# One partial product is copied into another's PSUM bank, where the second accumulates upon it; an addition on VectorE goes

## The chip, the cores and the metric

The kernel runs on one core of one Trainium2 chip. The metric is device time in microseconds (us): 2280.09 us is the median of three runs before the change (2279.85 to 2280.32). The core's engines are TensorE (PE in the rows; its loads of stationary operands are PEld), VectorE (DVE), ScalarE (ACT), GpSimd (POOL), and SyncE (SP), which issues the transfers. Each engine runs its own instructions in the order in which they were written and waits on semaphores for the others.

## The reference

The work is channel attention followed by a gated feed-forward layer, on 4 batches of 6080 tokens with 256 channels; the hidden width is 2048.

```python
qn = q / (norm(q, axis=1) + 1e-06);  kn = k / (norm(k, axis=1) + 1e-06)
s = kn.transpose(0, 2, 1) @ qn / tau          # 256 x 256 for each batch
a = softmax(s)                                # rows, in float32
x = (v @ a).reshape(B * S, 256)
h = x @ w_in                                  # 256 -> 2048
g = h * (1 / (1 + exp(-1.702 * h)))
out = g @ w_out                               # 2048 -> 256
```

The weights `w_in` and `w_out` arrive as float64 and are turned into float32 on the chip.

## The kernel before, in words

For each batch the kernel first forms the 256 x 256 attention matrix from q and k (class `Attention`; the next batch's is built while the present one is multiplied), multiplies it into `w_in` (`weights`, line 582), and then only has to form V x (a w_in) for the tokens. The tokens of a batch are cut into 12 chunks of 512 (the last has 448), the hidden width into 4 groups of 512. One chunk with one group is a **unit** (`unit`, line 684); there are 4 x 12 x 4 = 192.

All matrices are split into a high and a low part of a reduced float32 format (`F32R`), and each product is a sum of three matmuls: high x high, low x high, high x low. So a **product** is 2 x 3 = 6 matmuls with 256 columns, into the two halves of one PSUM bank (`product`, line 695).

V x W is done by a scheme with seven products in place of eight, M1 to M7. Their partial sums live in three kinds of banks: X (two of them in turn, `psX0` and `psX1`), Y and Z (one each). M1 opens X; M6, M5 and M3 are accumulated upon it in that order, and after M1, M6 and M5 ScalarE takes a copy of X to SBUF (`snap`: tiles `s1`, `u2`, `u4`). M2 opens Z. M7 opens Y and M4 accumulates upon it. Four quadrants of the hidden layer follow:

- first (c11): `s1` + Z, added by VectorE into `h1`, then the gate (Gelu) on ScalarE in SBUF (g11);
- second: X after M3, gated directly from PSUM (g12);
- third and fourth (c22, c21): Y + `u4` and Y + `u2` into `h2`, each then gated in SBUF.

Then `parts` (line 745) splits the gated `h1` and `h2` into `gh` (a cast, by ScalarE for `h1`, by VectorE for `h2`) and `gl` (a subtraction on VectorE), and eight groups of three 512-column matmuls into the output banks `ps_o` multiply them by `w_out` (line 776). Below, "output groups" are these.

The first batch differs: units run in pairs of chunks, and between them the weights of the next group are read, turned to float32 on VectorE (`to_float32`, line 285) and multiplied by the attention matrix. This is the start-up, to about 170 us into the span. `weights` there puts its two halves (`ps_w`) one after the other into the same bank, and the second waits until ScalarE has copied the first (`w1`).

The order on every engine is made by a planner (`Plan.order`, line 85): each operation is a node with an engine, an assumed cost, its predecessors and a due time, and each engine takes the ready node with the smallest due time. Slots (banks and tiles) are reused in the order in which the program asked for them. Whatever changes costs, predecessors or due times of a few nodes therefore moves instructions on all engines.

Of the kernel before, what the change touches and what calls it, by code (L numbers as in the profile page):

```python
# [15 lines left out]
ALU = mybir.AluOpType  # L16
# [4 lines left out]
P = 128  # L21
# [3 lines left out]
NCH = 512  # L25
# [138 lines left out]
def act(n, psum=False, pointers=0):  # L164
    return (165 if psum else 190) + 0.833 * n + 93 * pointers


def dve(n):
    return (151 + n) / 0.96
# [10 lines left out]
def channel_attention_then_glu(  # L180
# [10 lines left out]
    nc = tc.nc  # L191
# [21 lines left out]
    g = Plan()  # L213

    def sbuf(slot, shape, dtype=F32, name=None):
        return g.buf(slot, lambda: sb.tile(list(shape), dtype, tag=slot, name=name or slot))
# [4 lines left out]
    def bank(slot, name=None):  # L221
        return g.buf(slot, lambda: ps.tile([P, NCH], F32, tag=slot, name="ps_" + (name or slot)))
# [3 lines left out]
    ones = sb.tile([P, P], F32, name="ones")  # L226
# [7 lines left out]
    def two(ap, w):  # L234
        return ap.rearrange("p (a n) -> p a n", a=2)[:, :, :w]
# [6 lines left out]
    def cast(dst, src, n, deps, uses, due, psum=False):  # L242
        return g.add("ACT", act(n, psum), lambda: nc.scalar.copy(dst(), src()), deps, uses, due)  # L243
# [4 lines left out]
    def tt(dst, a, b, op, n, deps, uses, due):  # L248
        return g.add("DVE", dve(n), lambda: nc.vector.tensor_tensor(dst(), a(), b(), op=op), deps, uses, due)  # L249
# [329 lines left out]
    P1, P2, P3, P5, P7, P6, P4 = range(7)  # L579
# [98 lines left out]

    marks = []
    outs = {}

    def unit(W, V, b, c, grp, count, chunk_no):
        D = len(marks)
        due = 45.0 * D
        o, w = chunks[c]
        hw = w // 2
        wh, wl, w_ok = W
        vh, vl, v_ok = V  # L690
        X = bank(f"psX{D % 2}", "X")
        Y = bank("psY", "Y")
        Z = bank("psZ", "Z")

        def product(m, into, begin, due, deps):
            def fn():
                for a in range(2):
                    dst = into()[:, a * HALF : a * HALF + hw]
                    for n, (l, r) in enumerate(((wh, vh), (wh, vl), (wl, vh))):
                        nc.tensor.matmul(  # L700
                            dst, lhsT=l()[:, m, a, :], rhs=r()[:, m, :hw],
                            start=begin and a == 0 and n == 0, stop=True, skip_group_check=True,
                        )

            return g.add("PE", 6 * hw * 0.4427, fn, [*deps, *w_ok, v_ok[m]], [wh, wl, vh, vl, into], due)

        def snap(name, dep, due):
            s = sbuf(name, [P, 2, HALF], F32)
            n = cast(lambda: s()[:, :, :hw], lambda: two(X(), hw), w, [dep], [X, s], due, psum=True)
            return s, n  # L710

        h1 = sbuf(f"h1{D % 2}", [P, 2, NCH], F32, "h1")
        h2 = sbuf("h2", [P, 2, NCH], F32)
        left = lambda h: h()[:, :, :hw]
        right = lambda h: h()[:, :, hw:w]

        def gate(dst, src, deps, uses, due, psum):
            return g.add(
                "ACT", act(w, psum), lambda: nc.scalar.activation(dst(), src(), AF.Gelu_apprx_sigmoid),  # L719
                deps, uses, due,  # L720
            )

        m1 = product(P1, X, True, due, [])
        marks.append(m1)
        s1, s1n = snap("s1", m1, due + 4)
        m2 = product(P2, Z, True, due + 6, [])
        m6 = product(P6, X, False, due + 15, [s1n])
        u2, u2n = snap("u2", m6, due + 19)
        c11 = tt(lambda: left(h1), lambda: two(Z(), hw), lambda: s1()[:, :, :hw], ALU.add, w,
                 [s1n, m2], [Z, s1, h1], due + 11)  # L730
        g11 = gate(lambda: left(h1), lambda: left(h1), [c11], [h1], due + 24, False)
        m5 = product(P5, X, False, due + 27, [u2n])
        u4, u4n = snap("u4", m5, due + 31)
        m7 = product(P7, Y, True, due + 30, [])
# [102 lines left out]
    for b in range(B):  # L837
# [5 lines left out]
        for s, (c, grp) in enumerate(order):  # L843
            if grp == 0:
                chunk_no += 1
            due = 45.0 * len(marks)
            unit(W[grp], V[b, c], b, c, grp, s, b * NCHUNK + c)
            here = [marks[-1]]
            if b == 0 and s < 2 * NG:
# [75 lines left out]
```

## Time and profile before

| what | value |
|---|---|
| median of three runs | 2280.09 us |
| span of the profiled execution | 2281.3 us |
| TensorE busy | 2233.8 us (98%), 14036 matmuls |
| VectorE busy | 1528.0 us (67%) |
| ScalarE busy | 1309.9 us (57%) |
| GpSimd busy | 5.1 us |
| transfers | 118.59 MB, mean 52 GB/s |
| matmuls of the output groups, line 776 | 45% of the chain that ended last |
| matmuls of the seven products, line 700 | 40% of that chain |

The profiled execution has no other time of its own than its span, from its first to its last instruction. It is 1.2 us above the median of the runs. Busy times are sums over an engine's instructions; shares are of the span. The matmuls overlap one another in the records (a 512-column matmul is shown as about 390 ns, the next one starts some 228 ns after it), so a product's real pace is read from the distance between starts.

### The profile page before, as it was taken

The page shows a single profiled execution, that of the slowest core. Times are in us where ns is not written, and L with a number is a line of the kernel's source. Part 1 is how long each engine was busy: PE and PEld are TensorE (multiplying, and loading weights), DVE is VectorE, ACT ScalarE, POOL GpSimd, SP SyncE. Part 2 cuts the span into 40 slices and gives each one's busy share as a digit, 9 for nine tenths or more (in the row PEclk, how much of TensorE's full clock was granted, in tenths as well). Part 3 has the DMA queues.
Part 4 walks back from the last instruction along what each step waited for, and adds up shares of the span by engine and source line. Part 5 has one row for each costly group of instructions (what it writes and reads, how often), then busy time and mean ns, then how long its engine had stood idle before and what let it go on. Part 6 is the DMA issues. An engine that isn't in the chain of part 4 may idle for free.

```text
span 2281.3 us, 33938 instructions
## 1 busy us (share of the span) xinstructions
PE 2233.8 (98%) x14036; PEld 2026.0 (89%) x14036; DVE 1528.0 (67%) x2273; ACT 1309.9 (57%) x2198; POOL 5.1 (0%) x10
## 2 busy tenths in 40 slices
PE   9699999999999999999999999999999999999999
PEld 8579999998899999999899999999989899999998
DVE  7996766666586676666567666676657755656654
ACT  6556666665576566566456565565556554545553
POOL 0000000000000000000000000000000000000000
PEclk9899999999999999999999999999999999999999
DMA  7222122111021121111111121111101000100100
GB/s 274 88 70 75 47 76 74 47 52 39 28 73 38 56 74 48 47 38 54 37 31 61 38 78 53 56 38 66 34 29 47 30 25 19 38 19 19 36 10 18
DMA packets 60523, 118.59 MB, mean 52 GB/s; under 512 B 6096, under 2 KB 10192, under 8 KB 60368
## 3 DMA queue, kind: packets, MB, share of 16 engines
q1 hardware_dynamic: 60368, 116.42, 15.6%
q8 instruction: 110, 1.80, 0.3%
q14 instruction: 45, 0.37, 0.1%
HBM read 89.39 MB, written 27.00 MB: 51 GB/s over the span
## 4 chain that ended last, share of the span: by engine, by line
PE 92%; DVE 5%; ACT 1%; DMA 1%; issue 1%; SPq 0%; ACTq 0%
PE ps_o L776 45%; PE ps_X L700 23%; PE ps_Y L700 11%; PE ps_Z L700 6%; PE ps_s L466 5%; PE ps_w L613 2%; DVE h L249 1%; DMA v_raw<-in_vT 1%; DVE gl L254 1%; DVE acc_q L249 0%; DVE acc_k L249 0%; DVE low L327 0%; ACT h L719 0%; DMA raw_k<-in_k 0%; DVE wl L254 0%
## 5 line engine op out<-in xcount | busy, mean ns | idle before, releaser
L249 DVE TENSOR_TENSOR h<-ps_Y,u 128x512 f32<-128x512 f32 (+1 forms) x384 | 262.7, 684 | 617.8 <-PE ps_Y L700 509.2
L776 PE MATMUL ps_o<-gl,wo_h 128*128 128x512 f32 (+1 forms) x1536 | 597.1, 389 | 6.8 <-DVE gl L254 6.8
L776 PE MATMUL ps_o<-gh,wo_h 128*128 128x512 f32 (+1 forms) x1536 | 601.3, 391 | 0.9 <-ACT gh L243 0.9
L776 PE MATMUL ps_o<-gh,wo_l 128*128 128x512 f32 (+1 forms) x1536 | 600.2, 391 | 0.0
L254 DVE TENSOR_TENSOR gl<-h,gh 128x1024 fp32r<-128x1024 f32 (+1 forms) x384 | 464.9, 1211 | 30.6 <-ACT gh L243 25.1
L719 ACT ACTIVATE h<-h 128x512 f32<-128x512 f32 (+1 forms) x576 | 357.8, 627 | 150.9 <-DVE h L249 149.9
L700 PE MATMUL ps_X<-v_h,wh 128*128 128x256 f32 (+1 forms) x1536 | 435.0, 283 | 7.5 <-ACT s L243 3.0
L700 PE MATMUL ps_X<-v_l,wh 128*128 128x256 f32 (+1 forms) x1536 | 433.9, 283 | 0.0
L700 PE MATMUL ps_X<-v_h,wl 128*128 128x256 f32 (+1 forms) x1536 | 433.9, 282 | 0.0
L243 ACT COPY u<-ps_X 128x512 f32<-128x512 f32 (+1 forms) x384 | 221.8, 578 | 303.9 <-PE ps_X L700 303.0
L776 PEld LDWEIGHTS ps_o<-gl,wo_h 128*128 128x128 f32 x1536 | 289.6, 189 | 69.1 <-DVE gl L254 9.2
L719 ACT ACTIVATE h<-ps_X 128x512 f32<-128x512 f32 (+1 forms) x192 | 113.8, 592 | 387.9 <-PE ps_X L700 387.8
L776 PEld LDWEIGHTS ps_o<-gh,wo_h 128*128 128x128 f32 x1536 | 290.7, 189 | 48.9 <-ACT gh L243 1.1
L776 PEld LDWEIGHTS ps_o<-gh,wo_l 128*128 128x128 f32 x1536 | 291.0, 189 | 45.0
L700 PEld LDWEIGHTS ps_X<-v_h,wh 128*128 128x128 f32 x1536 | 293.7, 191 | 24.8 <-ACT u L243 4.7
L700 PEld LDWEIGHTS ps_X<-v_l,wh 128*128 128x128 f32 x1536 | 293.9, 191 | 11.7
L700 PEld LDWEIGHTS ps_X<-v_h,wl 128*128 128x128 f32 x1536 | 294.0, 191 | 0.0
L700 PE MATMUL ps_Y<-v_h,wh 128*128 128x256 f32 (+1 forms) x768 | 218.3, 284 | 4.9 <-DVE h L249 3.9
L700 PE MATMUL ps_Y<-v_h,wl 128*128 128x256 f32 (+1 forms) x768 | 216.7, 282 | 0.9 <-DVE wl L254 0.9
L700 PE MATMUL ps_Y<-v_l,wh 128*128 128x256 f32 (+1 forms) x768 | 216.6, 282 | 0.0
L243 ACT CAST gh<-h 128x1024 fp32r<-128x1024 f32 (+1 forms) x192 | 199.5, 1039 | 6.0
L700 PEld LDWEIGHTS ps_Y<-v_h,wh 128*128 128x128 f32 x768 | 147.0, 191 | 9.8 <-DVE h L249 5.0
(108 smaller groups left out, 2713.9 us busy)
## 6 DMA issues: line engine op xcount, KB each, us to landing
v_raw<-in_vT SPq DMA_DIRECT2D x44, 512.0 KB, 4.7
out_T<-osb SPq DMA_DIRECT2D x88, 256.0 KB, 2.0
raw_q<-in_q SPq DMA_DIRECT2D x69, 256.0 KB, 2.9
raw_k<-in_k SPq DMA_DIRECT2D x69, 256.0 KB, 3.3
wf<-win_f SPq DMA_DIRECT2D x24, 256.0 KB, 3.8
raw_q<-in_q SPq DMA_DIRECT2D x11, 512.0 KB, 5.8
raw_k<-in_k SPq DMA_DIRECT2D x11, 512.0 KB, 6.7
words<-in_w_in SPq DMA_DIRECT2D x8, 512.0 KB, 3.5
```

The lines of the kernel that those rows point to most:

```text
L243: return g.add("ACT", act(n, psum), lambda: nc.scalar.copy(dst(), src()), deps, uses, due)
L249: return g.add("DVE", dve(n), lambda: nc.vector.tensor_tensor(dst(), a(), b(), op=op), deps, uses, due)
L254: lambda: nc.vector.tensor_tensor(dst(), src(), hi().bitcast(F32), op=ALU.subtract),
L466: nc.tensor.matmul(out, lhsT=rk()[:pp, j, l, ci], rhs=rq()[:pp, j, r, :], start=begin and m == 0, stop=last and m == 2, skip_group_check=True,
L613: nc.tensor.matmul(pb(), lhsT=l()[:, j, ci], rhs=r()[:, j, :], start=n == 0, stop=n == 3 * NC2 - 1,)
L700: nc.tensor.matmul(dst, lhsT=l()[:, m, a, :], rhs=r()[:, m, :hw], start=begin and a == 0 and n == 0, stop=True, skip_group_check=True,)
L719: "ACT", act(w, psum), lambda: nc.scalar.activation(dst(), src(), AF.Gelu_apprx_sigmoid),
L776: nc.tensor.matmul(ob()[:, :w], lhsT=l[:, f, ds], rhs=rr()[:, a, :w], start=begin and m == 0, stop=end and m == 2,)
```

## The change

ScalarE's copy of X after M1 no longer goes to the SBUF tile `s1` but into the bank Z. M2 then no longer opens Z: its matmuls accumulate upon what ScalarE wrote, so Z holds M1 + M2. VectorE's addition c11 is gone, and the gate g11 reads Z in PSUM and writes `h1`. So that accumulation is defined for every element of the bank, four 128-column matmuls of ones write all of Z once at the program's start. M2 now has the copy as predecessor, and the copy has M1 and, through the slot, the gate g11 of the unit before. Due times: g11's goes from 24 to 11 after the unit's own.

```diff
+    zb = bank("psZ", "z")
+
+    def fn_z():
+        for i in range(NCH // P):
+            nc.tensor.matmul(
+                zb()[:, i * P : (i + 1) * P], lhsT=ones, rhs=ones, start=i == 0, stop=True, skip_group_check=True,
+            )
+
+    z_clean = g.add("PE", 880, fn_z, (), [zb], -9e8)
...
         m1 = product(P1, X, True, due, [])
         marks.append(m1)
-        s1, s1n = snap("s1", m1, due + 4)
-        m2 = product(P2, Z, True, due + 6, [])
+        s1n = cast(lambda: two(Z(), hw), lambda: two(X(), hw), w, [m1, z_clean], [X, Z], due + 4, psum=True)
+        m2 = product(P2, Z, False, due + 6, [s1n])
         m6 = product(P6, X, False, due + 15, [s1n])
         u2, u2n = snap("u2", m6, due + 19)
-        c11 = tt(lambda: left(h1), lambda: two(Z(), hw), lambda: s1()[:, :, :hw], ALU.add, w,
-                 [s1n, m2], [Z, s1, h1], due + 11)
-        g11 = gate(lambda: left(h1), lambda: left(h1), [c11], [h1], due + 24, False)
+        g11 = gate(lambda: left(h1), lambda: two(Z(), hw), [m2], [Z, h1], due + 11, True)
```

Three places of the new order matter below. The first is ScalarE at the beginning of the second batch (the same stands at the third and fourth), from the cast of the new attention matrix (`aT_h`) on. Before:

```order
L243 CAST aT_h_5586<-ps_t_5578 128x512
L243 COPY s1_5597<-ps_X_5590 128x512
L719 ACTIVATE h1_5599<-h1_5599 128x2x256
L243 COPY u2_5615<-ps_X_5590 128x512
L243 COPY s1_5617<-ps_X_5517 128x512
L243 COPY u4_5633<-ps_X_5590 128x512
```

and now:

```order
L243 CAST aT_h_5502<-ps_t_5494 128x512
L243 COPY ps_Z_5513<-ps_X_5506 128x512
L728 ACTIVATE h1_5527<-ps_Z_5513 128x2x256
L243 COPY ps_Z_5529<-ps_X_5433 128x512
L243 COPY u2_5531<-ps_X_5506 128x512
L728 ACTIVATE h1_5545<-ps_Z_5529 128x2x256
L243 COPY u4_5553<-ps_X_5506 128x512
```

The copy of M1, the gate of the finished sum and the copy of the next unit's M1 now stand one behind the other on the one bank Z, ahead of `u2`.

The second place is TensorE at the same point (M1 of that unit, then what follows it). Before, M6 and then the next unit's M2:

```order
L700 MATMUL ps_X_5590<-v_h_5004,wl_785 128x256
L700 MATMUL ps_X_5590<-v_h_5004,wh_772 128x256
...
L700 MATMUL ps_X_5590<-v_h_5004,wl_785 128x256
L700 MATMUL ps_Z_5608<-v_h_5004,wh_1045 128x256
L700 MATMUL ps_Z_5608<-v_l_5048,wh_1045 128x256
```

and now its own M2 at once, M6, and the next unit's M2:

```order
L709 MATMUL ps_X_5506<-v_h_4942,wl_799 128x256
L709 MATMUL ps_Z_5513<-v_h_4942,wh_786 128x256
...
L709 MATMUL ps_X_5506<-v_h_4942,wh_786 128x256
...
L709 MATMUL ps_Z_5529<-v_h_4942,wh_1055 128x256
L709 MATMUL ps_Z_5529<-v_l_4964,wh_1055 128x256
```

Before, the unit's M2 had been done before the attention matrix was ready; now it stands directly behind M1.

The third place is TensorE in the start-up, around the second half of a group's weights (`ps_w`). Before, four output groups follow it:

```order
L613 MATMUL ps_w<-win_h,aT_l 128x512 x2
L776 MATMUL ps_o<-gh,wo_h 128x512
L776 MATMUL ps_o<-gh,wo_l 128x512
L776 MATMUL ps_o<-gl,wo_h 128x512
...
L700 MATMUL ps_Y<-v_h,wh 128x256
```

and now M4 comes at once, and the next unit's M1 behind it:

```order
L613 MATMUL ps_w<-win_h,aT_l 128x512 x2
L709 MATMUL ps_Y<-v_h,wh 128x256
L709 MATMUL ps_Y<-v_l,wh 128x256
L709 MATMUL ps_Y<-v_h,wl 128x256
...
L709 MATMUL ps_X<-v_h,wh 128x256
```

All eight output groups of a unit now stand ahead of that half of the weights.

## Rows read from the trace of the kernel before

**Rows 1.** The page's first lines: span, busy time, share, instructions of the engines

```profile
span 2281.3 us, 33938 instructions
PE 2233.8 (98%) x14036; PEld 2026.0 (89%) x14036; DVE 1528.0 (67%) x2273; ACT 1309.9 (57%) x2198; POOL 5.1 (0%) x10
```

**Rows 2.** Stretches: bounds, length, busy us by engine, granted clock, transfers' share, GB/s

```profile
89.63:164.09 74.46, 66.03 (x373) 55.61 (x373) 73.19 (x125) 45.08 (x76) 0.00 (x0) 1.00 0.26 82
800.00:1000.00 200.00, 200.00 (x1294) 182.98 (x1293) 135.93 (x192) 118.97 (x198) 0.00 (x0) 1.00 0.18 59
```

**Rows 3.** Timeline, TensorE, one unit of the last batch: start, duration, engine, line, operation

```profile
2026.06 0.40 PE L776 MATMUL ps_o<-gh,wo_h 128*128 128x512 f32 x1
...
2031.53 0.28 PE L700 MATMUL ps_X<-v_h,wh 128*128 128x256 f32 x1
...
2036.56 0.40 PE L776 MATMUL ps_o<-gh,wo_h 128*128 128x512 f32 x1
```

**Rows 4.** Groups by line: busy us, mean ns of one, idle before and releaser

```profile
L249 DVE TENSOR_TENSOR h<-ps_Z,s 128x512 f32<-128x512 f32 (+1 forms) x192 | 130.7, 681 | 11.5 <-ACT s L243 10.0
L243 ACT COPY s<-ps_X 128x512 f32<-128x512 f32 (+1 forms) x192 | 111.1, 578 | 11.7 <-PE ps_X L700 11.3
L719 ACT ACTIVATE h<-h 128x512 f32<-128x512 f32 (+1 forms) x576 | 357.8, 627 | 150.9 <-DVE h L249 149.9
L719 ACT ACTIVATE h<-ps_X 128x512 f32<-128x512 f32 (+1 forms) x192 | 113.8, 592 | 387.9 <-PE ps_X L700 387.8
```

**Rows 5.** Timeline, ScalarE, the same unit: the gate after M3, then the cast

```profile
2032.44 0.60 ACT L719 ACTIVATE h<-ps_X 128x512 f32<-128x512 f32 x1 [3.59 <-PE ps_X L700]
2033.07 1.05 ACT L243 CAST gh<-h 128x1024 fp32r<-128x1024 f32 x1
```

**Rows 6.** Timeline, VectorE: c11 and the next instruction

```profile
2037.16 0.68 DVE L249 TENSOR_TENSOR h<-ps_Z,s 128x512 f32<-128x512 f32 x1
2037.76 0.68 DVE L249 TENSOR_TENSOR h<-ps_Y,u 128x512 f32<-128x512 f32 x1
```

**Rows 7.** VectorE in the start-up: c11 by tile, first and last start

```profile
L249 DVE TENSOR_TENSOR h<-ps_Z,s x6: 681/682/684, 84.6 to 150.0; 128x512 f32<-128x512 f32 x6
```

**Rows 8.** Timeline, start-up: a wait of VectorE, weights' second half, their split's last part

```profile
89.63 0.69 DVE L249 TENSOR_TENSOR h<-ps_Y,u 128x512 f32<-128x512 f32 x1 [0.57 <-ACT u L243]
...
100.26 0.73 PE L613 MATMUL ps_w<-win_h,aT_h 128*128 128x512 f32 x2 [1.29 <-ACT w L243]
...
105.71 1.22 DVE L254 TENSOR_TENSOR wl<-sx,wh 128x1024 fp32r<-128x1024 f32 x1
```

**Rows 9.** Timeline, beginning of the second batch: TensorE and ScalarE around M1

```profile
580.52 0.28 PE L700 MATMUL ps_X<-v_h,wl 128*128 128x256 f32 x1
580.84 0.58 ACT L243 COPY s<-ps_X 128x512 f32<-128x512 f32 x1 [1.79 <-PE ps_X L700]
...
581.47 0.39 PE L700 MATMUL ps_X<-v_h,wh 128*128 128x256 f32 x1 [0.68 <-ACT s L243]
...
583.34 0.39 PE L700 MATMUL ps_X<-v_h,wh 128*128 128x256 f32 x1 [0.16 <-ACT u L243]
...
589.24 0.38 PE L700 MATMUL ps_X<-v_h,wh 128*128 128x256 f32 x1 [0.29 <-ACT u L243]
```

**Rows 10.** Stretches at the beginning of the second batch, columns as in Rows 2

```profile
569.00:572.40 3.40, 1.30 (x7) 0.78 (x6) 3.26 (x8) 3.37 (x6) 0.00 (x0) 1.00 0.79 280
572.50:575.90 3.40, 3.40 (x9) 2.64 (x9) 1.93 (x5) 0.25 (x2) 0.00 (x0) 0.51 0.00 0
...
579.00:584.00 5.00, 3.47 (x24) 2.94 (x24) 1.58 (x3) 2.22 (x5) 0.00 (x0) 1.00 0.00 0
```

**Rows 11.** Timeline, TensorE at the head of the program

```profile
4.63 2.55 PE L460 MATMUL ps_s<-raw_q,raw_k 128*128 128x256 f32 x8
9.70 1.62 PE L460 MATMUL ps_s<-raw_q,raw_k 128*128 128x256 f32 x3 [2.52 <-DMA raw_k<-in_k]
```

## The prediction, made before the changed kernel ran

> **What bounds the kernel now.** The first lines of the page come first: TensorE is busy 2233.8 of 2281.3 us, VectorE 1528.0, ScalarE 1309.9 [rows 1]. Then the stretches, because a mean hides stages: from 800 to 1000 us TensorE is busy 200.00 of 200.00 at granted clock 1.00, while in the start-up, 89.63 to 164.09, it is busy 66.03 of 74.46 and VectorE 73.19 [rows 2]. So there are two regimes. In the steady one nothing but fewer or slower matmuls can move the end. In the start-up VectorE paces. Third come the single matmuls. One unit of the last batch runs from 2026.06 to 2036.56, 10.50 us; its 24 output matmuls take 5.47 (0.228 each), its 42 product matmuls, 2031.53 to 2036.56, take 5.03 (0.120 each), so a product takes 0.72 [rows 3]. The change takes none of these matmuls away: M2 has the same six, and only the flag by which the first opens the bank differs. Whatever it brings must come out of the stretches in which TensorE waits. Since VectorE's 192 additions (130.7 us [rows 4]) lie in steady time but for a few, most of that relief is worth nothing.
>
> **The change part by part.** All sums are made against the profiled span, 2281.3 us, which is 1.2 above the median of 2280.09; I take that 1.2 off at the end.
>
> *The addition c11, steady.* 192 times 681 ns of VectorE go. VectorE was busy 135.93 of 200 us there [rows 2], so 0.
>
> *The gate g11 out of PSUM.* A gate takes 592 ns from PSUM, 627 from SBUF [rows 4]: 192 x 0.035 = 6.7 us less on ScalarE, which was busy 118.97 of 200 [rows 2]: 0.
>
> *The four matmuls of ones.* No row shows them. The nearest are the first matmuls of the head, eight of 256 columns in 2.55 us, 0.32 each [rows 11]: 4 x 0.32 = 1.3 at most. They stand ahead of the wait for `raw_k`, which holds TensorE for 2.52 us until 9.70 [rows 11] and absorbs them: 0. Without that cover it would be 1.3.
>
> *c11 in the start-up.* Six instances lie between 84.6 and 150.0 [rows 7]. VectorE goes from one such instruction to the next in 0.60 (2037.16 to 2037.76 [rows 6]), so they hold 3.6 us of the engine that paces; with them may go a wait of 0.57 for ScalarE at 89.63 [rows 8]. At most 4.2 us come back.
>
> *What the new order gives back there.* In three groups of weights all eight output groups now stand ahead of the second half of `ps_w`, where before four followed it. That half therefore comes later by four groups of three matmuls: 12 x 0.228 = 2.73. Of this, 1.29 is covered by a wait that stood there before [rows 8] and 0.60 by a c11 less on VectorE: 0.84 stays, for three groups 2.5. TensorE then waits for the split of these weights: it ran from 100.26 to 105.71 + 1.22 = 106.93 [rows 8], 6.67 us, and only the half itself (about 1.4), M4 and the next M1 (0.72 each) stand in between, so it idles some 3 us in one piece, where before output groups filled the time. Start-up: -4.2 + 2.5 = -1.7. Bounds: -4.2, if nothing comes back; -4.2 + 3 x 2.73 = +4.0, if nothing is covered.
>
> *The clock in that idle time.* At the second batch TensorE was busy 1.30 of 3.40 us (569.0 to 572.4), and in the next 3.40 us the granted clock was 0.51 and nine matmuls ran [rows 10], 1.4 us more than 9 x 0.228 = 2.05. Against that, the start-up idled 8.43 us in all at a granted clock of 1.00 [rows 2]. I take half of one such fall, +0.7; bounds 0 and three falls, 4.1.
>
> *The first unit after the start-up.* Its M2 stands two products (1.44) behind M1's end. From M1's last matmul to the copy's start 0.32 passed (580.52 to 580.84), so 0.20 after the matmul's 0.12; the copy takes 0.58, and M6 began 0.05 after its end [rows 9]: 0.83. If ScalarE is in a cast of 1.05 [rows 5] as M1 ends, M2 starts up to 0.44 late; I take half, +0.2.
>
> *The beginnings of batches 2 to 4.* This is the main new wait. Before, M6 waited for the copy of M1 until 581.47 and M2 had been done earlier. Now M2 takes that place at 581.47, and ScalarE and TensorE alternate on Z. Between 581.47 and 583.34 less its wait of 0.16, two products took 1.71 [rows 9], 0.855 each, so M2 lasts to 582.33, M6 to 583.18. The gate starts at 582.53 and takes 0.59, the next unit's copy runs from 583.15 to 583.73, and the next M2 starts at 583.78: a new wait of 0.60. It ends at 584.50 and M5 starts, its copy `u2` done by 584.36. M5 began at 583.34 before with one product less (0.72) behind it: 0.44 late. By the next M5, at 589.24 before after a wait of 0.29 [rows 9], I put it at 0.6, since the same alternation recurs there. Three times 0.6 = +1.8. Bounds: 0, if later waits absorb it; 0.6 + 0.72 each, 4.0, if the place that M2 left is idle instead of filled.
>
> *Steady, the new chain on Z.* M2 now waits for a copy that waits for a gate. Counted in the new order with the paces of [rows 3], at least 7 us of matmuls stand between M1 and M2 in 112 of the 192 units; the tightest pattern with a loaded ScalarE comes 29 times: behind M3 follow M1, M4, another M1 and M7, then M2, so 4 x 0.72 = 2.87 us of matmuls. In that time ScalarE does the gate of M3 (0.20 and 0.63 to the next), the cast (1.05 [rows 5]) and the copy (0.58 + 0.05): 2.51. Slack 0.36: 0.
>
> Sum: -1.7 + 0.7 + 0.2 + 1.8 = +1.0. Span 2282.3; less 1.2, 2281.1 us.
>
> A page weighs on the copy. ScalarE's copy from PSUM to SBUF takes 578 ns [rows 4]; no row shows one into PSUM. The Trainium skill, "ScalarE: Activation LUTs", section "Step-by-step: what each stage is for", says that ScalarE writes PSUM faster than SBUF. No run here shows it yet; were it worth the 35 ns that reading shows, the two copies at each of three beginnings would give 0.2 us, and the sum would be 2280.9.
>
> **The rivals.**
>
> *VectorE's relief carries through.* The output groups that moved forward stay covered, so the start-up gives its whole 4.2; and at the batches' beginnings a c11 less (0.60 each) ahead of TensorE's idle time, in which VectorE was busy 3.26 of 3.40 [rows 10], cancels the 1.8 and ends the half-rate stretch. -4.2 + 0.2 - 2 x 1.35 (two of three stretches gone) = -6.7: 2273.4 us. For it speaks that VectorE is the busy engine in both places; against it that the new order makes TensorE idle in longer pieces.
>
> *The clock falls at the new waits; slower.* Six waits are new in kind: three for weights of about 3 us and three on Z. Without the 0.7 the sum is +0.3; each fall costs 1.35 (3.40 - 2.05 [rows 10]). Five falls give +7.1: 2287.1 us; it decides from the fourth on. For it speaks the fall behind 2.10 us of idle time in [rows 10]; against it that the 5.0 us from 579.0, busy 3.47 with several short waits, kept 1.00 [rows 10], and that lost speed of TensorE costs less where VectorE paces.
>
> The Trainium skill, "TensorE: Matmul & The Clock Gate", section "A second HAM failure mode: psum-queue depth-cycling", tells of a kernel in which short idle times between groups that cycle PSUM banks made the clock fall and recover again and again. By it the three alternations on Z alone would bring 3 x 1.35 = 4.1 and the time would be 2285.2. The trace disagrees for the short waits from 579.0 on and agrees only behind the longer idle time.
>
> *The copy into PSUM costs far more than 0.58; slower.* Each 0.1 above adds 0.6 at the beginnings (two copies, three times), and beyond the slack of 0.36 also 29 x 0.1 = 2.9. At twice the length, 1.16: 3.5 + 29 x 0.22 = 9.9 more, 2291.0 us. It decides from about 0.98 us. For it speaks only that no row shows this write; against it that the reading side differs by 35 ns.
>
> *The change doesn't do what it says:* M2 overwrites the copied M1. The time is the first case's.
>
> **How the numbers follow.** My forecast, little change: 0.67, its own range 2277.5 to 2284.5. VectorE's relief 0.09, clock falls 0.14, slow copy 0.08, overwriting 0.02. About 0.2% (4.6 us) can be told from no change here, so faster lies below 2275.5 and slower above 2284.65: faster 0.09, same 0.67 + 0.02 = 0.69, slower 0.14 + 0.08 = 0.22. The low end, 2276.0, is the start-up's -4.2 with +0.2 and nothing lost at the beginnings (2276.1). The high end, 2287.5, holds the start-up's worst bound (+5.7 to the sum, 2286.8) and five falls; the slow copy, the faster rival and six falls stay outside, 2 in 10.
>
> **What will show it.** c11 should be gone from VectorE's groups, 192 instances and about 130 us, with TensorE's busy time unchanged within 2 us. The copy `ps_Z<-ps_X` near 578 ns settles the third rival. At each of three beginnings M2 should be shown with two waits for ScalarE of about 0.7 and 0.6. In the start-up TensorE should wait about 3 us before products that use the second half of the weights, and the stretch up to the last start-up unit should be 1 to 2 us shorter; granted clocks below 0.9 there would be the second rival. In steady stretches TensorE must stay at 100%: a unit that takes more than 10.50 us with an M2 waiting for ScalarE makes the forecast wrong.

## The result, and the profile after

The changed kernel takes 2295.11 us, median of three runs (2293.24 to 2295.31), against 2280.09: a ratio of 1.0063, 95% interval 1.005 to 1.0077. It is slower by 15 us, where 2281.1 and no change were forecast and the range ended at 2287.5.

The page of the profile after, first lines, answering to [rows 1]:

```profile
span 2291.5 us, 33798 instructions
PE 2242.4 (98%) x14044; PEld 2029.1 (89%) x14044; DVE 1426.6 (62%) x2081; ACT 1310.9 (57%) x2198; POOL 5.1 (0%) x10
```

The spans differ by 10.2 us and the medians by 15.0, since neither profiled execution stands at its median. That of after took 2293.24 us, 1.9 below its median and 1.7 above its own span. If before's time lies as far above its span of 2281.3, it is 2283.0, which is 2.9 above the median and not 1.2. The head of before was slow: its first transposition of the attention matrix began 3.6 us later than after's, most of it the 2.52 us for `raw_k` [rows 11], which is a transfer and does not appear among the waits of after. Lengths of stretches are therefore compared below from that transposition on.

VectorE lost 101 us and TensorE *gained* 8.6 us of busy time, though it has only the four small matmuls of ones more (eight records in the trace). That is the first hint: the loss hides inside "busy".

The groups by line of after (columns as in [rows 4]): the copy into the bank, the copies into SBUF, and the gate from Z.

```profile
L243 ACT COPY u<-ps_X 128x512 f32<-128x512 f32 (+1 forms) x384 | 222.6, 580 | 353.5 <-PE ps_X L709 348.0
L243 ACT COPY ps_Z<-ps_X 128x512 f32<-128x512 f32 (+1 forms) x192 | 110.4, 575 | 38.2 <-PE ps_X L709 37.8
L728 ACT ACTIVATE h<-ps_Z 128x512 f32<-128x512 f32 (+1 forms) x192 | 113.2, 590 | 82.4 <-PE ps_Z L709 80.3 <-ACT u L243 1.8
```

A copy into PSUM costs 575 ns, one into SBUF 580: the rival of the slow copy is out. The Trainium skill ("ScalarE: Activation LUTs", "Step-by-step: what each stage is for") says that writes to PSUM are faster; here the difference is 5 ns.

The beginning of the third batch after (timeline; first the last matmul of M1, then copy, M2, gate, copy and next M2 in turn on Z):

```profile
1141.33 0.28 PE L709 MATMUL ps_X<-v_h,wl 128*128 128x256 f32 x1
1141.64 0.57 ACT L243 COPY ps_Z<-ps_X 128x512 f32<-128x512 f32 x1 [1.79 <-PE ps_X L709]
1142.26 0.38 PE L709 MATMUL ps_Z<-v_h,wh 128*128 128x256 f32 x1 [0.66 <-ACT ps_Z L243]
...
1143.34 0.60 ACT L728 ACTIVATE h<-ps_Z 128x512 f32<-128x512 f32 x1 [1.13 <-PE ps_Z L709]
...
1143.97 0.57 ACT L243 COPY ps_Z<-ps_X 128x512 f32<-128x512 f32 x1
...
1144.59 0.38 PE L709 MATMUL ps_Z<-v_h,wh 128*128 128x256 f32 x1 [0.63 <-ACT ps_Z L243]
```

Both waits that the prediction walked through, 0.68 and 0.60, are there with 0.66 and 0.63 (compare [rows 9]), and the list of TensorE's waits (total, times, longest) holds just these six of them:

```profile
PE ps_Z L709 <- ACT ps_Z L243: 3.9, 6, 0.7
```

Where the time went is in two other places. The first is steady time. Stretches of after, columns as in [rows 2], the start-up from the first transposition to the end of its last unit and then the steady stretch:

```profile
69.00:176.00 107.00, 93.94 (x499) 81.23 (x500) 90.79 (x155) 59.00 (x102) 0.00 (x0) 0.89 0.23 69
800.00:1000.00 200.00, 199.66 (x1277) 181.56 (x1276) 128.25 (x179) 119.52 (x199) 0.00 (x0) 1.00 0.18 59
```

TensorE is busy 199.66 of 200 us where it was 200.00 [rows 2], a shortfall of 0.2% that looks like nothing. The timeline of after shows what sits behind it (M4 ends, M1 of another unit, then M7):

```profile
935.45 0.28 PE L709 MATMUL ps_Y<-v_h,wl 128*128 128x256 f32 x1
...
935.77 0.69 DVE L249 TENSOR_TENSOR h<-ps_Y,u 128x512 f32<-128x512 f32 x1 [3.59 <-PE ps_Y L709]
935.92 0.58 ACT L243 COPY ps_Z<-ps_X 128x512 f32<-128x512 f32 x1
...
936.17 0.28 PE L709 MATMUL ps_X<-v_h,wl 128*128 128x256 f32 x1
936.38 1.22 DVE L254 TENSOR_TENSOR gl<-h,gh 128x1024 fp32r<-128x1024 f32 x1
...
936.52 0.38 PE L709 MATMUL ps_Y<-v_h,wh 128*128 128x256 f32 x1
936.74 0.28 PE L709 MATMUL ps_Y<-v_l,wh 128*128 128x256 f32 x1
```

M7 reopens bank Y, and VectorE's sum c21 still reads M4's result out of Y; VectorE's next instruction starts at 936.38. M7 starts at 936.52, 0.35 after the matmul ahead of it where 0.12 is the pace, and the matmul behind it 0.22 later: 0.33 lost. No wait is printed, because the record of the matmul ahead lasts until 936.45: only 0.07 of the loss is idle time in the profile (five such places are the 0.34 that TensorE is short of 200.00). The rest shows only in distances between starts. There are 27 such places after the start-up, 8.9 us in all, against 6 and 1.9 us in the trace of before.

The second place is the start-up. First transposition and first output group of the seventh unit, before:

```profile
69.72 0.66 PE L566 MATMUL ps_t<-ident,x 128*128 128x128 f32 x2 [9.02 <-DVE x L557]
...
175.81 0.40 PE L776 MATMUL ps_o<-gh,wo_h 128*128 128x512 f32 x1
```

and after:

```profile
66.12 1.09 PE L566 MATMUL ps_t<-ident,x 128*128 128x128 f32 x4 [9.02 <-DVE x L557]
...
177.42 0.40 PE L783 MATMUL ps_o<-gh,wo_h 128*128 128x512 f32 x1
```

106.09 us have become 111.30: 5.2 longer. The stretch of before from 69 to 176 had the clock at 0.94, where after's has 0.89:

```profile
69.00:176.00 107.00, 92.52 (x515) 78.68 (x516) 97.51 (x171) 61.84 (x105) 0.00 (x0) 0.94 0.23 73
```

In after, TensorE stands for the new weights (timeline), and three stretches are at the lower of the two clock levels, 1.2 GHz. One comes behind the wait shown; the wait for the weights of the group before, 1.83 us at 102.08, was followed by none, and the other two come behind 2.46 us for `wh` at 77.8 and behind 1.43 and 1.17 us ahead of an output group at 158.6 and 160.5:

```profile
130.11 0.35 PE L709 MATMUL ps_X<-v_h,wh 128*128 128x256 f32 x1 [1.95 <-DVE wl L254]
...
131.34 0.39 PE L709 MATMUL ps_Y<-v_h,wh 128*128 128x256 f32 x1 [0.28 <-ACT wh L243]
...
132.60 0.58 PE L709 MATMUL ps_Y<-v_h,wl 128*128 128x256 f32 x1 [0.76 <-DVE wl L254]
```

```profile
79.60:82.80 3.20, 3.20 (x16) 3.20 (x16) 3.03 (x7) 1.80 (x3) 0.00 (x0) 0.50 0.59 226
...
132.90:136.00 3.10, 3.10 (x16) 3.10 (x16) 3.04 (x5) 0.62 (x1) 0.00 (x0) 0.50 0.37 85
160.90:166.70 5.80, 5.80 (x19) 4.83 (x19) 3.96 (x7) 0.57 (x1) 0.00 (x0) 0.50 0.01 3
```

Before had one such stretch there (84.6 to 87.8). Taking each matmul's pace above its full-rate pace (0.228 and 0.120), after loses 6.8 us to them and before 1.4: 5.4, about the 5.2 by which the start-up grew. The gaps between starts that are longer than the pace by over 0.1 add up to 19.1 us in both traces. TensorE waits elsewhere, but not longer; what is lost is lost at the lower clock.

### The profile page after: what moved, and what is told of

Same layout as the page of the kernel before. It is cut to its first block, busy times and chain, and to the rows that moved or that the text cites. A ratio compares the mean times of both kernels' runs of the same rounds, so it can differ in the third digit from the quotient of the medians.

```text
span 2291.5 us, 33798 instructions
## 1 busy us (share of the span) xinstructions
PE 2242.4 (98%) x14044; PEld 2029.1 (89%) x14044; DVE 1426.6 (62%) x2081; ACT 1310.9 (57%) x2198; POOL 5.1 (0%) x10
## 4 chain that ended last, share of the span: by engine, by line
PE 91%; DVE 5%; ACT 2%; DMA 1%; issue 0%; SPq 0%; ACTq 0%
PE ps_o L783 45%; PE ps_X L709 22%; PE ps_Y L709 12%; PE ps_Z L709 6%; PE ps_s L466 5%; PE ps_w L613 2%; DVE h L249 1%; ACT h L728 1%; DVE gl L254 1%; DMA v_raw<-in_vT 1%; ACT gh L243 1%; DVE acc_k L249 0%; DVE acc_q L249 0%; DMA raw_k<-in_k 0%; DVE low L327 0%
## 5 line engine op out<-in xcount | busy, mean ns | idle before, releaser
L728 ACT ACTIVATE h<-h 128x512 f32<-128x512 f32 (+1 forms) x384 | 239.6, 624 | 117.1 <-DVE h L249 116.7
L728 ACT ACTIVATE h<-ps_Z 128x512 f32<-128x512 f32 (+1 forms) x192 | 113.2, 590 | 82.4 <-PE ps_Z L709 80.3
```

## The experiments

There are three theories. **Theory 1:** the loss is M7's wait for bank Y, brought by the order of TensorE's instructions and not by the data path. **Theory 2:** it is the copy into PSUM and the accumulation upon it. **Theory 3:** the start-up's new order is a second loss. The kernel before had a median of 2280.53, 2280.07 and 2280.45 us beside the first four experiments, the next three and the last.

| run | median us | ratio to before, 95% interval | start-up, us | clock 69 to 176 |
|---|---|---|---|---|
| before | 2280.1 to 2280.5 | | 106.09 | 0.94 |
| after | 2295.11 | 1.0063 [1.005, 1.0077] | 111.30 | 0.89 |
| e1 order alone | 2286.93 | 1.0031 [1.0019, 1.0043] | 106.58 | 0.94 |
| e2 Y free | 2285.73 | 1.0023 [1.0014, 1.0032] | 110.76 | 0.88 |
| e3 M7 behind M2 | 2296.00 | 1.007 [1.0058, 1.0083] | 107.60 | 0.95 |
| e4 M1 early | 2285.98 | 1.0028 [1.0018, 1.0038] | 109.15 | 0.90 |
| e5 start-up alone | 2282.98 | 1.0016 [1.0007, 1.0024] | 110.58 | 0.90 |
| e6 start-up undone | 2281.39 | 1.0008 [0.9999, 1.0017] | 106.52 | 0.93 |
| e7 start-up held | 2281.66 | 1.0008 [0.9999, 1.0017] | 106.37 | 0.93 |
| e8 before, M7 later | 2282.44 | 1.0007 [0.9998, 1.0016] | 105.53 | 0.95 |

The start-up is the distance shown above, from the first transposition to the first output group of the seventh unit, in one trace each.

**e1, the order without the data path** (in the kernel before):

```diff
-        m2 = product(P2, Z, True, due + 6, [])
+        m2 = product(P2, Z, True, due + 6, [s1n])
```

> The kernel before with one more predecessor: M2 waits for the copy of M1, though it still opens its own bank and VectorE still adds the two. This gives nearly the new order without any write of ScalarE into a bank. Theory 1 (the loss is M7's wait for bank Y, where M7 stands only one product behind the M4 of the unit before): 30 such places against 8 before, 0.33 us each, 22 x 0.33 = 7.3 us, so about 2287. Theory 2 (the loss is in the copy into PSUM and the accumulation upon it): within 2 us of 2280.

2286.93 us. Its trace has 27 waits of M7 for Y, 8.9 us, with M1 still copied to SBUF, M2 opening its own bank and c11 in place. Theory 1 holds, and theory 2 does not explain a loss that comes without the copy into PSUM.

**e2, Y taken out of the wait** (in the changed kernel):

```diff
-        c21 = tt(lambda: left(h2), lambda: two(Y(), hw), lambda: u2()[:, :, :hw], ALU.add, w,
+        c21 = tt(lambda: left(h2), lambda: u2()[:, :, :hw], lambda: u2()[:, :, :hw], ALU.add, w,
```

> The changed kernel in its own order, but the sum c21 adds u2 to u2 and no longer reads bank Y, so M7 of the next unit finds Y free (M4's result is left out of the output). Theory 1: the 27 waits of 0.33 us that the trace shows go, 8.9 us, so about 2286. Theory 2: no change, 2295.

2285.73 us: 9.4 us came back with TensorE's order untouched. (The sum now reads nothing that M4 wrote, so VectorE no longer waits for M4 either; e4 is free of this second change.) In the steady stretch (as above) TensorE no longer has a gap:

```profile
800.00:1000.00 200.00, 200.00 (x1286) 182.67 (x1286) 128.32 (x180) 119.84 (x201) 0.00 (x0) 1.00 0.18 59
```

**e3, M7 moved behind M2:**

```diff
-        m7 = product(P7, Y, True, due + 30, [])
+        m7 = product(P7, Y, True, due + 30, [m2])
```

> The changed kernel with M2 as a predecessor of M7 in each unit, so that M7 stands behind M2: 3 places with one product between M4 and the next M7 in place of 36. Theory 1: about 2286, unless M2 then waits for its copy in place of M7 for its bank, which would give back up to 0.36 us in each place (2.51 us of ScalarE against 2.15 us of matmuls) and leave the time at 2295. Theory 2: 2295.

2296.00 us, no better than after. None of the 27 waits is left, and the condition named in the expectation came true in part. The timeline of e3 at one of these places, from ScalarE's cast to M2:

```profile
795.70 1.05 ACT L243 CAST gh<-h 128x1024 fp32r<-128x1024 f32 x1
...
796.65 0.58 ACT L243 COPY ps_Z<-ps_X 128x512 f32<-128x512 f32 x1
...
796.91 0.28 PE L709 MATMUL ps_X<-v_h,wl 128*128 128x256 f32 x1
...
797.28 0.39 PE L709 MATMUL ps_Z<-v_h,wh 128*128 128x256 f32 x1
797.50 0.28 PE L709 MATMUL ps_Z<-v_l,wh 128*128 128x256 f32 x1
```

The copy had to queue behind the cast until 796.65, and M2 starts 0.37 after the matmul ahead in place of 0.12; with the next step 0.36 is lost. The place has two answers to wait for, VectorE on Y and ScalarE on Z, and both are late. M2 is late in this way at 17 places, 6.0 us in all, so two thirds of the 8.9 us are lost again. M7 now comes later, and TensorE's waits for VectorE's split ahead of the output groups grew too (after, then e3: total, times, longest):

```profile
PE ps_o L783 <- DVE gl L254: 7.9, 5, 2.1
...
PE ps_o L783 <- DVE gl L254: 13.2, 10, 2.7
```

(That the totals of e3 and after agree within 1 us is partly chance: e3's start-up was 3.7 us shorter, but it had half-rate stretches at all three beginnings.)

**e4, M1 earlier:**

```diff
-        m1 = product(P1, X, True, due, [])
+        m1 = product(P1, X, True, due - 3.5, [])
```

> The changed kernel with M1 due 3.5 us earlier in the plan, so that it stands ahead of the M3 of the unit before: 9 places with one product between M4 and M7 in place of 36, and the copy of M1 comes ahead of the gate and the cast on ScalarE. Theory 1: 27 x 0.33 = 8.9 us less, about 2286, with no wait for the copy in steady time. Theory 2: 2295.

2285.98 us, 9.1 less than after, now with both answers in time: M1 ahead of M3 lets the copy pass ahead of gate and cast, and M2, M6 and M7 follow M4. Stretches of e4:

```profile
69.00:176.00 107.00, 93.28 (x502) 81.66 (x503) 91.31 (x156) 59.95 (x102) 0.00 (x0) 0.90 0.22 69
800.00:1000.00 200.00, 200.00 (x1285) 182.64 (x1284) 129.12 (x179) 118.53 (x199) 0.00 (x0) 1.00 0.18 59
```

Steady time is whole again; the start-up is not.

**e5 and e6, the start-up alone and undone** (`D` counts the units. Shown is e5, which is the kernel before from the ninth unit on; e6 is e4 with `D >= 8` in its place. c11 and g11 switch by the same test):

```diff
+    NEW = lambda D: D < 8
...
+        if NEW(D):
+            s1n = cast(lambda: two(Z(), hw), lambda: two(X(), hw), w, [m1, z_clean], [X, Z], due + 4, psum=True)
+            m2 = product(P2, Z, False, due + 6, [s1n])
+        else:
+            s1, s1n = snap("s1", m1, due + 4)
+            m2 = product(P2, Z, True, due + 6, [])
```

> The kernel before, with the change in its first eight units alone (the start-up). Theory 3 (the start-up of the changed order is the second loss: waits for the second half of the weights and the half-rate stretches behind them, 5.2 us between the first transposition of the attention matrix and the seventh unit in the traces): about 2280.5 + 5 = 2285.5. Rival (the start-up only varies from run to run, or VectorE's relief shows there): 2279 to 2281.

> The change with M1 due 3.5 us earlier (as in e4), but the first eight units keep the copy to SBUF and VectorE's addition. Theory 3: e4's 2286.0 less 5 us, about 2281. Rival (what is left in e4 lies in steady time or at the beginnings of the batches): 2286.

2282.98 and 2281.39 us. Put in alone, the new start-up costs 2.9 us by the medians (interval 1.6 to 5.5), less than the 5 expected; taken out of e4 it gives back 4.6. The sign is the expected one in both. The traces say 110.58 and 106.52 us for the start-up. The lower clock goes with the order: behind the transposition's own stretch, four traces without output groups behind the second half of the weights (after, e2, e4, e5) lose 6.6 to 7.0 us to it, and the five in which four groups still follow that half (before, e1, e6, and e7 and e8 below) 1.3 to 3.9. Only e3, which has the new order but M7 elsewhere, stands between: it loses 2.7 us to the clock, and its gaps are 1.6 us longer than in after.

**e7, the new data path with the old order in the start-up** (as e4; `held` lists the second four output groups of each unit, `pw[1][1]` is the second half of the weights):

```diff
+        for x in held.get(len(marks) - 2, []) if len(marks) <= 6 else []:
+            x.deps = [*x.deps, pw[1][1]]
```

> As e4, with the change in all units, but in the start-up the second four output groups of every other unit are held until the second half of the next group's weights, as they stood in the kernel before. Theory 3 with the order as its cause: the waits for these weights and the half-rate stretches go, so about 2281, and less, down to 2277, if VectorE's relief (4.2 us) then shows. Rival (the copy on Z itself is what slows the start-up): 2286.

2281.66 us: as good as e6, with Z and the gate from PSUM in every unit. Its start-up against that of after above:

```profile
69.00:176.00 107.00, 94.22 (x521) 81.86 (x522) 93.50 (x160) 63.45 (x107) 0.00 (x0) 0.93 0.22 69
```

So the start-up's loss, too, lies in the order. VectorE's relief (4.2 us at most) does not show in the length: 106.37 us against 106.09, with VectorE busy 93.50 in place of 97.51. A part of it is there. TensorE's gaps from the transposition on add up to 17.7 us in place of 19.1, but half-rate pace takes 2.1 us more than in before.

**e8, the same lever on the kernel before:**

```diff
-        m7 = product(P7, Y, True, due + 30, [])
+        m7 = product(P7, Y, True, due + 30, [m6])
```

> The kernel before with M6 as a predecessor of M7, so that 3 places in place of 8 have one product between M4 and the next M7. Theory 1 holds for the kernel before too: its six waits of 0.33 us for bank Y (2.0 us in its trace) go, about 2278.5, unless M7 then waits with M6 for the copy of M1. Rival (these waits cost nothing there): 2280.

2282.44 us, not faster (interval -0.5 to +3.7 us). One of the six waits for Y is left, but two other waits are longer. M6 waits for the copy of M1, 7.3 us in e8 against 3.0 (4 times, 1.0 at most) in before, and what was added lies in the start-up, which was no longer for it (105.53 us). The output groups wait for VectorE's split, 9.6 us against 6.8 (4 times, 2.1 at most), and this lies at the batches' beginnings (three waits of 2.66 in place of 2.10) and behind them (three of 0.40 that are new). That is more than the 1.6 us that the waits for Y give back:

```profile
PE ps_o L776 <- DVE gl L254: 9.6, 7, 2.7
...
PE ps_X L700 <- ACT s L243: 7.3, 6, 2.9
```

No version found beats the kernel before.

## Why the prediction was wrong

By medians, the 15.0 us are: 9.1 for the waits on Y (after to e4), 4.6 for the start-up (e4 to e6), and 1.3 left. But e4 and e6 have none of the six waits for Y that before has, so against before these waits explain 7.0 (8.9 less 1.9), and 3.2 are left.

**What bounds the kernel: right in kind.** Nothing came of VectorE's 130 us. But from "TensorE busy 200.00 of 200.00" it was concluded that nothing but fewer or slower matmuls could move the end. It is the opposite: where TensorE has no idle time, every product that comes a little too early for its bank is paid in full.

**The step that failed first: "Steady, the new chain on Z ... Slack 0.36: 0".** The pattern was named (M3, M1, M4, M1, M7, M2, 29 times), and only M2's chain through ScalarE was followed in it. The slack held: in after M2 never waits there. But M2 had moved behind M7, and so M7 had moved from two products behind M4 to one: 36 places in the trace of after in place of 9 (the expectations count 8). Two numbers that show it to be too close stood in the rows. From a bank's last matmul to the reader's start passes 0.32 [rows 9], and VectorE's pace is 0.60 [rows 6]: 0.92 from the start of M4's last matmul. One product between gives 0.12 + 0.72 = 0.84, two give 1.56. That says that M7 comes 0.08 too early, so the sign could have been had; the size could not, for the trace shows M7 late by 0.23 and the step behind it by another 0.10. The step asked who waits in the new chain, and not who moved forward because of it.

**The step that failed second: the start-up, -1.7 + 0.7.** Measured +5.2 in the trace, 3 to 5 by medians. That weights would be waited for was right for two of the three groups: 2.9 and 3.0 us, but in three pieces each (1.95, 0.28 and 0.76 in the one shown above), where the prediction's own figures (6.67 less 1.4 and twice 0.72) give 3.8. Yet these waits only took the place of others, since the gaps add up to 19.1 us before and after. The failed term is the clock's. "Half of one fall, +0.7" was too little: three half-rate stretches instead of one cost 5.4 us. The argument against it, that lost speed of TensorE costs less where VectorE paces, did not hold. The rival of the clock falls had the mechanism in the start-up, but not its other half on Z.

**The beginnings of the batches, +1.8: about right.** The waits came to 0.66 and 0.63. In the profiled execution they don't show as a loss: twelve units around the second beginning took 138.24 us in place of 138.76, but only because TensorE's idle time of 2.1 us was not followed by a half-rate stretch, as it was before [rows 10]. That is luck. e5, which has the order of before there, took 137.13 and 137.15 us at the two beginnings where its clock did not fall, and e4, without the waits for Y, 137.50: 0.36 more, and 0.69 more when the 0.33 for Y that e5 still has in these units is taken out. The forecast was 0.6. The Trainium skill ("TensorE: Matmul & The Clock Gate", "A second HAM failure mode: psum-queue depth-cycling") tells of a kernel whose short idle times between groups that cycle PSUM banks made the clock fall again and again. The alternation on Z does not bear that out here; it ran at granted clock 1.00:

```profile
1141.00:1146.00 5.00, 3.71 (x29) 3.30 (x28) 0.00 (x0) 2.59 (x5) 0.00 (x0) 1.00 0.01 3
```

**Gate and copy: right.** 590 and 575 ns, and M2 does accumulate upon ScalarE's data. The four matmuls of ones, put at 1.3 us at most and covered by the wait for `raw_k`, take 1.7 us in after (eight records), where that wait does not appear at all:

```profile
4.62 1.86 PE L685 MATMUL ps_z<-ones 128*128 128x128 f32 x8
6.32 42.28 PE L460 MATMUL ps_s<-raw_q,raw_k 128*128 128x256 f32 x192
```

No cost shows behind them: the first transposition starts at 66.1 to 68.3 us in the traces that have them and at 67.1 to 69.7 in those that don't. No experiment priced them.

**What is left.** In the last batch a unit takes 10.52 us (2035.21 to 2045.73) in place of 10.50 [rows 3]:

```profile
2035.21 0.40 PE L783 MATMUL ps_o<-gh,wo_h 128*128 128x512 f32 x1
...
2045.73 0.40 PE L783 MATMUL ps_o<-gh,wo_h 128*128 128x512 f32 x1
```

The eight output groups stand there in two blocks of four, where before they were one block. e1 keeps the block and 10.50 (36 units in 377.95 us against 377.89 before), and the kernels with two blocks take 378.66 for the 36: 0.02 a unit, 1.0 over 48. With 0.69 at each of three beginnings that is 3.1 of the 3.2 us left. So close an agreement is partly chance: e6's median is uncertain by about 2 us either way, and the falls of the clock at the beginnings, which come and go, are not in this sum.

## What to carry to other kernels

When a new dependence delays one instruction on an in-order engine, look at what is scheduled in its place: the instruction that moves forward meets its own bank too early, and on an engine without idle time this is paid in full. Before moving work that reuses a single buffer, write down for each buffer the distance from last use to next opening against the reader's latency, for every chain at that place and not for the new one alone. And read gaps of a few tenths from the distances between starts: overlapping records show most of them as busy time.

## What the hardware showed that was not expected

Half-rate stretches do not come back at the same place: behind the same idle time of 2.10 us ahead of an output group, the clock fell to half in all three batches of before and in none of after; in e4 it fell at one beginning of three. By matmul pace a stretch of 3.4 us there costs about 1.5 us. By the time of twelve units it costs 1.6 in the order of before (138.76 against 137.15) and 2.3 in e4 (139.83 against 137.50). Part of the spread between executions of one kernel (2278.3 to 2281.3 us for before beside e1 to e4) may be of this kind; that was not shown.
